# One array layout (64 rows by 32 columns, two lanes) for the matmuls of an attention-plus-MLP kernel

## The chip, the cores and the metric

The kernel runs on one core of a Trainium2 chip. The metric is device time in microseconds of one execution; the number shown is the median of three runs. One further execution was recorded by the hardware profiler, and all views of the profile come from it. The engines are TensorE (PE in the profile; its weight loads are listed as PEld), ScalarE (ACT), VectorE (DVE), GpSimd (POOL) and SyncE (SP, which here only issues DMAs).

## The reference

The input `x` has 2048 tokens of 640 features. It is layer-normed, and the result `xn` feeds two branches whose outputs are added to `x`:

```python
xn = layernorm(x)                              # 2048 x 640
# A: 32 query heads of 20 features, one shared key head and one shared value head
scores = (xn @ wq per head) @ (xn @ wk).T * 20 ** -0.5
o = softmax(scores) @ (xn @ wv);   a = concat(o) @ wo
# B
b = silu(xn @ w1) @ w2                         # 640 -> 1728 -> 640
out = x + a + b
```

The scores are 32 heads x 2048 queries x 2048 keys, some 134 million exponentials; they are never stored, only their product with the values is.

## The kernel before

**Tiling of attention.** The queries are cut into 4 chunks of 512 (`QW`), the heads into 8 groups of 4 (`HG`). That gives 32 groups `g`, and each meets 16 key tiles `kt` of 128 keys. One unit of work is one head of one (g, kt): a score matmul with K = 20 features padded to 32, giving 128 keys x 512 queries in one PSUM bank (`s_mm`, line 1002; the matmul has the line L1003 in the profile). There are 32 x 16 x 4 = 2048 such units. The exponential of a unit goes one of two ways:

- on ScalarE, two or three units in one instruction over neighbouring banks (`make_s_act`, line 1057; the exponential is L1094). One matmul pass with the values then follows per (g, kt) (`make_pv_act`).
- on VectorE, always the four heads of a (g, kt), called a *batch* (`dve_items`, `dve_job`, `dve_advance`). The exponential is built by integer arithmetic on the bf16 bit pattern: four instructions that move a bank to SBUF (L1285, named p1), one shifted copy on VectorE (L1326), one on GpSimd (L1321). The three variants are added up by three value passes in place of one.

A value pass (`pv_mms`, L1129) is four matmuls, one for each head, side by side in the columns of the array; all accumulate in PSUM bank 7 (`UB`) until the group is complete, then VectorE copies the sum out (L1177).

**Dense work.** The q projections (`q_job`), the first MLP layer (`h_job`, `h_pair`; tanh on ScalarE, L709, product on VectorE, L712), and the second layer together with the output projection (`out_job`, `y_job`, and `fin_job` at the end) use `col_mm` (L395): four matmuls of 32 output columns each, side by side, repeated over chunks of the contracted dimension into one bank.

**Layouts of the array.** A matmul names its place in the 128 x 128 array. Three layouts occur, called modes in the code:

- "s": 32 rows x 128 columns, for the scores. Up to four heads run at once.
- "p": 128 rows x 32 columns, for values and dense work. The four side-by-side matmuls run at once.
- "f": the whole array, for transposes, k, v and the first q, mostly in the first 50 us.

**The order.** The program is not written out by hand. A planner (`Sched`, `step_pe`, `pe_candidates`, `plan`) steps through a modelled time and always commits the next instruction of the engine that is furthest behind. The matmul engine has a list of candidates: scores for ScalarE ("s"), scores for VectorE ("d"), values ("p", and "pd" for batches), dense jobs ("m", "l"). The planner holds costs (`t_mc`, `t_act`, `t_dve`) and `SWITCH`, the price of a change of layout; a table of rules chosen by a letter for each 10 us (`RULES`, `PLAN`) alters its thresholds. The finished order is fixed at build time; `emit` adds semaphore waits, one semaphore for each engine, and none from TensorE to itself. Work is shared between ScalarE and VectorE by the planner too: a batch is claimed (`claim`) when VectorE can be given one. PSUM has 8 banks, one for the values and seven for scores and dense jobs; exponentials wait in `Ebuf` (`NSLOT` = 20 slots of 512 columns).

**The start and the end.** The first scores need kT, which is written by one copy per job (`kT_job`, L566 and L568) into `kT_rep`: the same keys four times, once for each head's 32 rows. After the last exponential come the last value passes, the normalization of the last group through two small matmul stages (L924 and L942), the `fin_job` passes (L395) and the last additions (L891).

Of the kernel before, what the change touches and what calls it, by code (L numbers as in the profile page):

```python
# [8 lines left out]
BF16 = mybir.dt.bfloat16  # L9
# [5 lines left out]
P = 128  # L15
# [4 lines left out]
SLOT = 32  # L20
HG = 4
NG = H // HG
# [17 lines left out]
NSLOT = 20  # L40
# [4 lines left out]
NQS = 3  # L45
# [4 lines left out]
WAITS = 0.0  # L50
BUSY = 0.5
STRETCH = 2400.0
FILLGAP2 = 120.0
FILL = 0.7
WARM = 2400.0
# [14 lines left out]
SWITCH = 105.0  # L70
# [7 lines left out]
FIN_ACT = ()  # L78
# [10 lines left out]
BASE = dict(lagmax=6, lagp=0, lagj=6, openlag=3, late=-0.02, lead=0.01, leadmax=0.02, need=500.0, hold=300.0, dwant=600.0, slack=700.0, dnow=400.0, hungry=0.0, patience=0.0, keep=460.0, open=2, zcap=9, stay=0.0, homes=1, last=6, twin=2, spare=300.0, want=1, claim=6)  # L89
RULES = dict(a={}, b=dict(keep=0.0), c=dict(lagp=3), d=dict(lagp=5), e=dict(lagp=0), f=dict(patience=200.0), g=dict(dwant=0.0),  # L90
             h=dict(zcap=4), i=dict(zcap=3), j=dict(homes=0), k=dict(leadmax=-1.0, lead=-1.0), l=dict(lead=0.08, leadmax=0.1),
             m=dict(need=560.0), n=dict(hold=0.0), o=dict(stay=460.0), p=dict(open=1), q=dict(slack=400.0), r=dict(hungry=1000.0), s=dict(claim=9), t=dict(open=3), u=dict(claim=4), v=dict(want=2), w=dict(twin=0), x=dict(need=440.0), y=dict(last=9), z=dict(last=6, hungry=1000.0))
PLAN = "bcbngdnvnroonapqndntaiaoinqqahppinxaaopfcfahhprpppopddmimdqahjqooafogaa"


def rule(n):
    return PLAN[n] if n < len(PLAN) else "a"
# [13 lines left out]
class Op:  # L111
    __slots__ = ("eng", "fn", "occ", "lat", "pre", "reads", "writes", "prio", "mode", "slots",
                 "start", "fin", "done", "deps", "inc", "job", "first", "last", "gate", "on_commit", "seq", "name",
                 "dma_sem", "dma_val", "port", "run")

    def __init__(self, eng, fn, occ, lat=0.0, pre=(), reads=(), writes=(), prio=5.0, mode=None, slots=None,
# [10 lines left out]
        self.slots = slots  # L127
# [12 lines left out]
        self.run = None  # L140
# [10 lines left out]
def t_mc(n):  # L151
    return n / 2.4 + (9.0 if n >= 512 else 4.0)
# [6 lines left out]
class Job:  # L159


    def __init__(self, name, cost):
        self.name = name
        self.cost = cost
        self.bank = None
        self.mms = deque()
        self.consumers = []
        self.ready = None
        self.fixed = None
        self.head = None  # L170
        self.batch = None


class Piece:


    def __init__(self, job, mms=None):
        self.job = job
        self.mms = deque(job.mms if mms is None else mms)
        self.gate = job.gate  # L180
        self.kind = None


class Sched:
    ENG = ("pe", "act", "dve", "pool", "sp")

    def __init__(self):
# [4 lines left out]
        self.pe_set = None  # L192
# [22 lines left out]
    def est(self, op):  # L215
# [6 lines left out]
        if op.slots is not None and self.joined(op) is not None:  # L222
            t = self.pe_set[0] + 4.0 * len(self.pe_set[1])
# [10 lines left out]
    def joined(self, op):  # L234

        if op.slots is None or self.pe_set is None or op.slots & self.pe_set[1] or self.t["pe"] > self.pe_set[2] + 1.0:
            return None
        return self.pe_set[0]

    def commit(self, op, start):  # L240
        e = op.eng
        op.deps = self.hazards(op)
        op.start = start
        if e == "pe":
            if op.mode != self.pe_mode:
                start += SWITCH + (10.0 if op.mode == "p" and self.pe_mode != "s" else -3.0 if op.mode == "p" else 0.0)
                self.pe_mode = op.mode
            s0 = self.joined(op)
            if s0 is not None:
                end = max(start + op.occ, self.pe_set[2])  # L250
                self.pe_set = (s0, self.pe_set[1] | op.slots, end)
                op.fin = start + op.occ + (142.0 if op.run else 170.0)
                op.occ = end - self.t[e]
                self.t[e] = end
            else:
                op.fin = start + op.occ + (142.0 if op.run else 170.0)
                self.t[e] = start + op.occ
                self.pe_set = (start, op.slots, start + op.occ) if op.slots else None
# [21 lines left out]
def build(nc, A_x, A_wq, A_wk, A_wv, A_wo, B_x, B_w1, B_w2, out, stack):  # L280
# [33 lines left out]
    kT_rep = sb([P, S], BF16)  # L314
# [76 lines left out]
    def col_mm(pe, b, n, w, x, start, stop, off=0):  # L391

        ins = None
        for j in range(w.shape[-1] // SLOT):
            ins = pe.matmul(ps[j * SLOT:(j + 1) * SLOT, b * BANK + off:b * BANK + off + n], w[:, j * SLOT:(j + 1) * SLOT], x,  # L395
                            start=start, stop=stop, tile_position=(0, j * SLOT))
        return ins

    def pe_job(name, mms, cost, gate=None):

        job = Job(name, cost)
        for k, (fn, occ, mode, pre, reads) in enumerate(mms):
            op = Op("pe", fn, occ, pre=pre, reads=reads, mode=mode, job=job, name=name)
            op.first = k == 0
            op.last = k == len(mms) - 1
            job.mms.append(op)
        job.ops = list(job.mms)
        job.ready = job.ops[-1]
# [21 lines left out]
    pool(lambda g: g.memset(mhalf[:, :], -0.5), 120, writes=[res("mh")], prio=0.03)  # L430
    idb = pool(lambda g: g.tensor_copy(ident_b[:, :], ident_f[:, :]), 290, reads=[res("idf")], writes=[res("idb")],
# [1523 lines left out]
```

## Time and profile before

| what | value |
|---|---|
| median of three runs | 706.66 us (706.38 to 706.92) |
| span of the profiled execution | 704.7 us |
| PE busy | 688.3 us, 98% |
| ACT busy | 683.8 us, 97% |
| DVE busy | 618.6 us, 88% |
| POOL busy | 363.6 us, 52% |
| matmuls / weight loads | 9915 / 9915 |
| exponentials on ScalarE | 665 instructions (583 of two units, 82 of three) |
| batches on VectorE | 159 |

The span of the profiled execution is 2.0 us under the median of the runs. How to read the views: a group row gives line, engine, operation, shapes and count, then the busy time and the mean duration of one, then the idle time just before them and what ended it. Instructions of an engine overlap at their ends, so that the mean duration is more than the step from one start to the next. For a matmul the shape "32*128" is rows times columns of the array that it uses. A timeline row gives start and length in us; neighbouring instructions of one group are merged, with their count behind the x.

### The profile page before, as it was taken

Reading aid. Unit: us, or ns where it says so; the run is one execution under the profiler, and the core shown is the slowest. Engines: PE = TensorE matmul, PEld = TensorE weight load, DVE = VectorE, ACT = ScalarE, POOL = GpSimd, SP = SyncE. Lnnn points to the kernel's source line nnn. Section 1 sums busy time; section 2 is a strip of 40 time slices with the busy share of each in tenths; the row PEclk is TensorE's granted clock in tenths of the full one; section 3 lists DMA queues with packets and bytes.
Section 4 is the critical chain, followed back from the end, with each engine's and each line's share of the span. In section 5 each row is a group of like instructions: output and inputs, shape, how many; then the busy total and the mean of one; then the engine's idle time right before and its main releaser. Section 6 shows DMA issues by size and latency. Waiting matters only on the chain.

```text
span 704.7 us, 22677 instructions
## 1 busy us (share of the span) xinstructions
PE 688.3 (98%) x9915; PEld 231.3 (33%) x9915; DVE 618.6 (88%) x1067; ACT 683.8 (97%) x737; POOL 363.6 (52%) x235
## 2 busy tenths in 40 slices
PE   7999999999999999999999999999999999999998
PEld 5432323222223333322222333332222333333345
DVE  7789999999998998889988899898999898889893
ACT  6999999999999999999999999999999999999993
POOL 6625544565565555445545446565554555455551
PEclk9999999999999999999999999999999999999999
DMA  8643220322221122323112222033222112232201
GB/s 222 196 145 40 21 19 19 31 29 26 21 24 16 29 40 30 65 28 33 17 19 29 28 31 30 19 62 43 30 20 20 18 21 33 28 68 24 21 8 39
DMA packets 34241, 28.97 MB, mean 41 GB/s; under 512 B 15486, under 2 KB 29662, under 8 KB 34142
## 3 DMA queue, kind: packets, MB, share of 16 engines
q1 hardware_dynamic: 33854, 27.20, 25.2%
q8 instruction: 77, 1.26, 0.8%
q10 hardware_dynamic: 288, 0.33, 0.1%
q14 instruction: 22, 0.18, 0.1%
HBM read 11.09 MB, written 2.62 MB: 19 GB/s over the span
## 4 chain that ended last, share of the span: by engine, by line
ACT 65%; PE 31%; DVE 2%; DMA 1%; POOL 0%; issue 0%; SPq 0%; POOLq 0%
ACT sbt L1094 63%; PE psall L1003 10%; PE psall L1129 10%; PE psall L395 9%; ACT sbt L709 3%; DMA sbt<-in_A_wq_dram 1%; PE psall L558 0%; PE psall L1608 0%; PE psall L924 0%; PE psall L942 0%; DVE sbt L500 0%; PE psall L670 0%; DVE sbt L1285 0%; DVE sbt L891 0%; PE psall L532 0%
## 5 line engine op out<-in xcount | busy, mean ns | idle before, releaser
L1094 ACT ACTIVATE sbt<-psall 128x1024 bf16<-128x1024 f32 (+1 forms) x665 | 661.2, 1223 | 3.4 <-PE psall L1003 2.9
L1285 DVE TENSOR_SCALAR sbt<-psall 128x512 int16<-128x512 f32 x636 | 417.2, 683 | 57.3 <-PE psall L1003 54.0
L1321 POOL TENSOR_SCALAR sbt<-sbt 128x2048 int16<-128x2048 int16 x159 | 302.0, 1899 | 300.0 <-DVE sbt L1326 116.2
L1003 PE MATMUL psall<-sbt 32*128 32x512 bf16 x2048 | 269.0, 384 | 7.6 <-ACT sbt L1094 3.8
L1129 PE MATMUL psall<-sbt 128*32 128x512 bf16 x3320 | 263.2, 384 | 1.6 <-DVE sbt L1177 1.1
L395 PE MATMUL psall<-sbt 128*32 128x320 bf16 (+3 forms) x3904 | 232.0, 331 | 0.3 <-DVE sbt L712 0.3
L1003 PEld LDWEIGHTS psall<-sbt 32*128 32x128 bf16 x2048 | 70.9, 91 | 254.0 <-ACT sbt L1094 189.5
L1326 DVE TENSOR_SCALAR sbt<-sbt 128x2048 int16<-128x2048 int16 x159 | 110.2, 704 | 1.8
L395 PEld LDWEIGHTS psall<-sbt 128*32 128x32 bf16 (+1 forms) x3904 | 83.9, 95 | 83.7 <-issue 51.6
L1129 PEld LDWEIGHTS psall<-sbt 128*32 128x32 bf16 x3320 | 66.1, 94 | 113.7 <-issue 79.8
L789 POOL TENSOR_TENSOR sbt<-sbt 128x512 bf16<-128x512 f32 x30 | 38.3, 1276 | 11.9 <-DVE sbt L1326 8.5
L712 DVE SCALAR_TENSOR_TENSOR sbt<-sbt,psall 128x512 bf16<-128x512 bf16 x52 | 35.5, 682 | 3.0 <-ACT sbt L709 2.6
L709 ACT ACTIVATE sbt<-psall 128x512 bf16<-128x512 f32 x52 | 37.8, 727 | 0.0
L1177 DVE COPY sbt<-psall 128x512 f32<-128x512 f32 x31 | 21.1, 680 | 0.1
L1608 PE MATMUL psall<-sbt 128*32 128x256 bf16 (+1 forms) x308 | 19.1, 338 | 1.2 <-DVE sbt L424 1.2
L630 DVE TENSOR_SCALAR sbt<-psall 128x512 bf16<-128x512 f32 x20 | 13.7, 685 | 1.2 <-PE psall L395 0.7
L831 DVE SCALAR_TENSOR_TENSOR sbt<-psall,sbt 128x320 bf16<-128x320 f32 x24 | 11.6, 482 | 0.5 <-PE psall L395 0.4
L522 POOL TENSOR_SCALAR sbt<-sbt 128x640 bf16<-128x640 bf16 x12 | 10.4, 879 | 2.5 <-DVE sbt L514 2.4
L1608 PEld LDWEIGHTS psall<-sbt 128*32 128x32 bf16 x308 | 8.2, 105 | 6.0 <-issue 2.5
L846 DVE SCALAR_TENSOR_TENSOR sbt<-psall,sbt 128x320 f32<-128x320 f32 x8 | 3.9, 485 | 6.4 <-PE psall L395 6.3
L532 PE MATMUL psall<-sbt 128*128 128x128 bf16 x80 | 7.1, 221 | 1.6 <-DVE sbt L525 1.1
L509 POOL TENSOR_TENSOR sbt<-sbt 128x2 f32<-128x2 f32 x8 | 5.6, 694 | 5.8 <-DVE sbt L507 5.7
(61 smaller groups left out, 98.9 us busy)
## 6 DMA issues: line engine op xcount, KB each, us to landing
sbt<-sbt SPq DMA_DIRECT2D x120, 64.0 KB, 3.9
sbt<-in_A_x_dram SPq DMA_DIRECT2D x28, 160.0 KB, 4.1
sbt<-sbt SPq DMA_DIRECT2D x213, 20.0 KB
out_dram<-sbt SPq DMA_DIRECT2D x14, 160.0 KB, 2.0
sbt<-in_B_w_dram SPq DMA_DIRECT2D x1, 2160.0 KB, 10.4
sbt<-in_B_w_dram SPq DMA_DIRECT2D x1, 2080.0 KB, 8.1
sbt<-sbt SPq DMA_DIRECT2D x75, 8.0 KB
sbt<-in_A_wq_dram SPq DMA_DIRECT2D x1, 800.0 KB, 6.7
```

What stands on the lines that cost most here:

```text
L395: ins = pe.matmul(ps[j * SLOT:(j + 1) * SLOT, b * BANK + off:b * BANK + off + n], w[:, j * SLOT:(j + 1) * SLOT], x, start=start, stop=stop ...
L709: t = Op("act", lambda a: a.activation(t_buf[0:rows, ts, :], bk(job.bank, 0, QW, rows=rows), AF.Tanh, scale=0.5), t_act(512), 215, pre=[jo ...
L712: u = Op("dve", lambda v: v.scalar_tensor_tensor(out=hT[par][0:rows, fk, :], in0=t_buf[0:rows, ts, :], scalar=1.0, in1=bk(job.bank, 0, QW, ...
L789: nm = pool(lambda e: e.tensor_tensor(oU[:, us, :], U_sb[:, us, :], Rrep, ALU.mult), 1350.0 + MARGIN, pre=[uc] + lc + pack_op.get(divmod(g ...
L1003: return pe.matmul(bk(b), kT_rep[i * SLOT:(i + 1) * SLOT, kt * P:(kt + 1) * P], qT[i * SLOT:(i + 1) * SLOT, g % NQ, :], start=True, stop=T ...
L1094: return a.activation(Ebuf[:, es * QW:es * QW + w], ps[:, buf[0] * BANK:buf[0] * BANK + w], AF.Exp, scale=ESCALE)
L1129: ins = pe.matmul(ps[i * SLOT:(i + 1) * SLOT, UB * BANK:UB * BANK + QW], lhsT, rhs, start=(first and k < HG), stop=(last and k >= len(lst) ...
L1177: uc = Op("dve", lambda v: v.tensor_copy(U_sb[:, us, :], bk(UB)), t_dve(512), 140, pre=[pv] + up, reads=[sc.banks[UB]], writes=[res("U", u ...
L1285: p1 = Op("dve", lambda v: v.tensor_scalar(z16[:, i * QW:(i + 1) * QW], bk(job.bank), ZBIAS, 0.0, ALU.add, ALU.max), t_dve(QW), 140, pre=[ ...
L1321: op = pool(lambda v, t=t, j=j, zin=zin: v.tensor_scalar(t.bitcast(I16), zin, float(SHIFT[j]), 1.0, ALU.add, ALU.mult), POOL_SHIFT, prio=0 ...
L1326: op = dve(lambda v, t=t, j=j, zin=zin: v.tensor_scalar_add(t.bitcast(I16), zin, float(SHIFT[j])), t_dve(N, 4), prio=SPRIO - 0.01 * j, **args)
L1608: ins = pe.matmul(ps[i * SLOT:(i + 1) * SLOT, UB * BANK:UB * BANK + n], zero_t[:, 0:SLOT], zero_t[:, 0:n], start=fresh, stop=fresh, tile_p ...
```

## The change

All score, value and dense matmuls use one layout: 64 rows x 32 columns. The array then has two *lanes* (the upper and the lower 64 rows, `rg` 0 and 1) of four column places each.

- **Scores.** A unit becomes four matmuls of 32 keys each, in the lane that holds its head (heads 0 and 1 in lane 0, heads 2 and 3 in lane 1). As a lane holds two heads' rows, kT is kept twice (`kT_ab`): one copy has zeros in the rows of the odd heads, the other in those of the even ones. A mask multiplies the copies in; the second copy waits for the first, as both read one bank.
- **Values and dense work.** Each pass of four matmuls becomes two half passes, over the upper and the lower 64 rows of the contracted dimension, in lanes 0 and 1.
- **Two lanes and one bank.** Both lanes add into the same bank for a value group or a dense job. Where the lane changes, the planner puts a wait of TensorE on its own earlier matmul (`blocked`, `selfwait`); TensorE has two semaphores for that, one for each lane.
- **The planner.** `rgfree` holds when each lane is free. Values stay in one lane until it is `runmax` half passes ahead. ScalarE is given two units at a time (`tri=0`); at most two banks wait for VectorE (`dmax=2`). `RULES`, `PLAN`, the twin sets and the fillers between scores are gone. `fin_job` passes are pieces of two half passes each.
- **Memory.** `NSLOT` 20 to 18, `NQS` 3 to 2.
- **Small work.** The zeroing of the ragged rows of `hT` on GpSimd goes; the last MLP chunk uses only the lane that holds data; VectorE zeroes a strip of `oT` and writes the mask.

```diff
-NSLOT = 20
+NSLOT = 18
-NQS = 3
+NQS = 2
-SWITCH = 105.0
+SWITCH = 100.0
+BASE = dict(lagmax=6, lead=0.01, leadmax=0.02, open=2, zcap=9, last=6, claim=6, dmax=2, runmax=4, linger=240.0, tri=0, need=700.0)
...
 def t_mc(n):
-    return n / 2.4 + (9.0 if n >= 512 else 4.0)
+    return n / 2.4 + 3.0
...
+    def blocked(self, op, bank):
+        w = self.acc.get(bank)
+        return w if w is not None and w.rg != op.rg else None
...
-    def col_mm(pe, b, n, w, x, start, stop, off=0):
+    def col_mm(pe, b, n, h, w, x, start, stop, off=0):
         ins = None
+        lo, hi = h * HROW, (h + 1) * HROW
         for j in range(w.shape[-1] // SLOT):
-            ins = pe.matmul(ps[j * SLOT:(j + 1) * SLOT, ...], w[:, j * SLOT:(j + 1) * SLOT], x,
-                            start=start, stop=stop, tile_position=(0, j * SLOT))
+            ins = pe.matmul(ps[j * SLOT:(j + 1) * SLOT, ...], w[lo:hi, j * SLOT:(j + 1) * SLOT], x[lo:hi],
+                            start=start, stop=stop, tile_position=(lo, j * SLOT))
...
+        for k in range(2):
+            args = dict(pre=[*job.ready, *mask_ops] + ops, writes=[res("kT", i, k) for i in range(t0, t1)], job=job)
+            if t0 == 1 or k == 1:
+                op = Op("dve", lambda v, k=k: v.tensor_scalar_mul(dst[:, k, :], bk(job.bank, 0, n), mask[:, k:k + 1]), ...)
+            else:
+                op = Op("act", lambda a, k=k: a.activation(dst[:, k, :], bk(job.bank, 0, n), AF.Copy, scale=mask[:, k:k + 1]), ...)
+            ops.append(op)
...
     def s_mm(pe, b, g, kt, i):
-        return pe.matmul(bk(b), kT_rep[i * SLOT:(i + 1) * SLOT, kt * P:(kt + 1) * P],
-                         qT[i * SLOT:(i + 1) * SLOT, g % NQ, :], start=True, stop=True, tile_position=(i * SLOT, 0))
+        r = slice(i // 2 * HROW, (i // 2 + 1) * HROW)
+        for c in range(P // SLOT):
+            k = kt * P + c * SLOT
+            ins = pe.matmul(bk(b)[c * SLOT:(c + 1) * SLOT], kT_ab[r, i % 2, k:k + SLOT], qT[r, g % NQ, :], start=True, stop=True,
+                            tile_position=(i // 2 * HROW, c * SLOT))
+        return ins
...
+        u = u_lane[0]
+        near = [min((e for _, e in x.values()), default=1e12) for x in pv]
+        if (near[u] > t + ru.linger or (pv_ahead[0] if u else -pv_ahead[0]) >= ru.runmax) and near[1 - u] <= t + ru.linger:
+            u = u_lane[0] = 1 - u
...
+        if not pro and xbanks() and dve_held(t) < ru.dmax:
+            for r in range(2):
+                dj = dve_items(r)
...
+            w = sc.blocked(op, bank) if bank is not None else None
+            if w is not None:
+                e = max(e, w.fin + LAT)
...
+        order = ["s", "m0", "d"] + (["p", "pd", "m", "l"] if lag_now() >= ru.lagmax else ["m", "p", "pd", "l"])
+        best = min(rd, key=lambda x: (order.index(x[0]), x[2])) if rd else None
```

More of the change, by code (lines that the diff above doesn't have):

```diff
@@ L242, in commit @@
         op.deps = self.hazards(op)
+        if op.selfwait is not None:
+            op.deps.add(op.selfwait)
         op.start = start
@@ L550, in build, with kT_res @@
     kT_op = {}
+    def kT_res(kt):
+        return [res("kT", kt, k) for k in range(2)]
     def kT_job(t0, t1):
@@ L1214, in z_idle @@
         b = z_last[k]
-        return b is None or b["pv"] is not None and all(o.done for o in b["pv"])
+        return b is None or b["pv"] is not None and all(o.done for x in b["pv"] for o in x)
     def z_slot():
@@ L1255, in dve_items @@
                 open_b.append(st)
-                pick = next(((st, j) for j in st["left"] if j not in busy), None)
-        if pick is None and open_b:
-            pick = open_b[0], open_b[0]["left"][0]
+                pick = next(((st, j) for j in st["left"] if j // 2 == r), None)
         if pick is None:
@@ L1811, in emit @@
                     continue
-                if d.eng == e and e == "pe":
+                if d.eng == e and e == "pe" and d is not op.selfwait:
                     continue
```

747 lines of the change are left out of this document (336 added, 411 removed).

## The prediction

> **What bounds the kernel now.** I read the page's busy shares first, then the groups with shapes kept apart, the stages, the waits, and last the timeline of single stretches.
>
> ```profile
> PE 688.3 (98%) x9915; PEld 231.3 (33%) x9915; DVE 618.6 (88%) x1067; ACT 683.8 (97%) x737; POOL 363.6 (52%) x235
> ```
>
> ```profile
> L1094 ACT ACTIVATE sbt<-psall 128x1024 bf16<-128x1024 f32 x583 | 565.8, 1174 | 0.7 <-PE psall L1003 0.5
> L1285 DVE TENSOR_SCALAR sbt<-psall 128x512 int16<-128x512 f32 x636 | 417.2, 683 | 57.3 <-PE psall L1003 54.0
> ...
> L1003 PE MATMUL psall<-sbt 32*128 32x512 bf16 x2048 | 269.0, 384 | 7.6 <-ACT sbt L1094 3.8 <-DVE sbt L1285 0.7 <-ACT sbt L568 0.3
> L1129 PE MATMUL psall<-sbt 128*32 128x512 bf16 x3320 | 263.2, 384 | 1.6 <-DVE sbt L1177 1.1 <-DVE sbt L1326 0.2 <-ACT sbt L1094 0.2
> L1094 ACT ACTIVATE sbt<-psall 128x1536 bf16<-128x1536 f32 x82 | 127.5, 1573 | 2.7 <-PE psall L1003 2.4
> L395 PE MATMUL psall<-sbt 128*32 128x512 bf16 x1468 | 114.5, 383 | 0.3 <-DVE sbt L712 0.3
> L395 PE MATMUL psall<-sbt 128*32 128x320 bf16 x2320 | 114.5, 301 | 0.0
> ```
>
> ```profile
> 50.00:200.00 150.00, 147.89 (x1918) 44.58 (x1910) 141.97 (x235) 149.08 (x172) 79.15 (x44) 1.00 0.23 25
> 200.00:350.00 150.00, 146.84 (x2114) 46.39 (x2111) 134.16 (x221) 149.93 (x159) 79.27 (x45) 1.00 0.25 32
> 350.00:500.00 150.00, 148.95 (x2118) 46.49 (x2118) 132.60 (x220) 150.00 (x162) 79.11 (x44) 1.00 0.25 32
> 500.00:650.00 150.00, 147.45 (x2214) 49.02 (x2206) 132.53 (x218) 149.97 (x160) 78.36 (x47) 1.00 0.24 29
> ```
>
> The columns of the stages are length, PE, PEld, DVE, ACT, POOL, clock and DMA. ScalarE never rests from 200 to 650 us, so the time falls only if it gets fewer exponentials, that is, if VectorE takes more batches. VectorE has room: 399.3 of 450 us there. The groups say why it rests: 54.0 of the 57.3 us before p1 (L1285) go to scores that TensorE has not delivered.
>
> And TensorE has no time to deliver them:
>
> ```profile
> 300.15 0.39 PE L1003 MATMUL psall<-sbt 32*128 32x512 bf16 x2
> 300.47 0.40 PE L1129 MATMUL psall<-sbt 128*32 128x512 bf16 x4
> 300.70 0.39 PE L395 MATMUL psall<-sbt 128*32 128x512 bf16 x4
> 301.02 0.39 PE L1003 MATMUL psall<-sbt 32*128 32x512 bf16 x3
> ```
>
> ```profile
> 160.13 1.26 PE L1129 MATMUL psall<-sbt 128*32 128x512 bf16 x20
> ```
>
> ```profile
> PEld psall L1003 <- ACT sbt L1094: 189.5, 496, 1.2
> ...
> PEld psall L1129 <- issue: 79.8, 352, 0.2
> PEld psall L395 <- issue: 51.6, 227, 0.4
> PEld psall L1003 <- issue: 31.0, 93, 0.5
> ```
>
> Five value passes of four matmuls take 1.26 us, the last 0.38 of it being one matmul's length: a step of 0.22 per pass. But from the scores at 300.15 to the next layout it is 0.32, and from the pass at 300.70 back to scores 0.32 again: 0.10 more each time. The waits count the changes: 496 + 93 = 589 entries into the score layout and 352 + 227 = 579 out of it, 1168 x 0.10 = 117 us. With scores (some 600 sets x 0.22 = 132), values (830 passes x 0.22 = 183), dense (367 x 0.22 + 580 x 0.14 = 162) and the whole-array work that is 610 us, and the smaller rows of waits hold more changes. TensorE, ScalarE and the order are all at their limit at once.
>
> **The change, part by part.** Durations are of the profiled execution (704.7 us); the median of the runs is 2.0 us above it, and I add that at the end.
>
> ```profile
> L532 PE MATMUL psall<-sbt 128*128 128x128 bf16 x80 | 7.1, 221 | 1.6 <-DVE sbt L525 1.1 <-DVE sbt L630 0.5
> L558 PE MATMUL psall<-sbt 128*128 128x512 bf16 x15 | 3.9, 382 | 0.0
> L582 PE MATMUL psall<-sbt 128*128 128x32 bf16 x80 | 2.6, 176 | 0.0
> L605 PE MATMUL psall<-sbt 128*128 128x128 bf16 x20 | 1.8, 220 | 0.7 <-DVE sbt L544 0.6
> ```
>
> ```profile
> 13.12 0.39 PE L1003 MATMUL psall<-sbt 32*128 32x512 bf16 x3
> 13.45 0.66 PE L582 MATMUL psall<-sbt 128*128 128x32 bf16 x20
> 13.56 1.45 ACT L1094 ACTIVATE sbt<-psall 128x1536 bf16<-128x1536 f32 x1 [0.63 <-PE psall L1003]
> ```
>
> ```profile
> 689.56 0.39 PE L1003 MATMUL psall<-sbt 32*128 32x512 bf16 x3
> ...
> 694.50 1.95 PE L942 MATMUL psall<-sbt 128*32 128x128 f32 x64
> 696.27 5.10 PE L395 MATMUL psall<-sbt 128*32 128x128 bf16 x144
> ```
>
> *TensorE's sum.* The changes of layout go, save those of the first 50 us. A unit of scores now fills a lane of its own for one pass, so 2048 units need 2048 / 2 x 0.22 = 225 us, where sets of three or four heads needed 132. Values and dense work stay at 183 and 162: twice the half passes, two at a time. With some 15 us of whole-array work (the first four rows) the sum is 585 us. Scores run from 13.1 to 689.6 us, 676 us. TensorE would be busy 87% of that. So about 13% comes free, provided that both lanes can be kept at work; the first rival is that they can't.
>
> ```profile
> 50.52 0.46 PE L1003 MATMUL psall<-sbt 32*128 32x512 bf16 x4
> ```
>
> That two sets in different rows may start at different times, which the lanes need, is seen here, too: four score matmuls in 0.46 us, where one takes 0.39, so the later ones started some 0.07 late into a running array.
>
> ```profile
> 88.99 3.84 ACT L1094 ACTIVATE sbt<-psall 128x1024 bf16<-128x1024 f32 x4
> 92.71 0.62 ACT L709 ACTIVATE sbt<-psall 128x512 bf16<-128x512 f32 x1
> 93.19 3.81 ACT L1094 ACTIVATE sbt<-psall 128x1024 bf16<-128x1024 f32 x4
> ```
>
> ```profile
> 299.74 1.29 DVE L1285 TENSOR_SCALAR sbt<-psall 128x512 int16<-128x512 f32 x2 [0.59 <-PE psall L1003]
> ```
>
> *More batches (the gain).* On ScalarE four exponentials of two units step from 88.99 to 92.71, 0.93 each, so four heads cost 1.86 us. On VectorE two p1 take 1.29, one 0.68: a step of 0.61, and a batch of four p1 and a shift 5 x 0.61 = 3.05. A batch that moves shortens the span by 1.86 and fills 3.05 of VectorE, so r us of recovered idle time move r / 4.91 batches. At most r = 54 (11 batches, 20.5 us). Nearest below: the stage from 50 to 200 us, where VectorE is at 94.6%; bringing the 450 us after it from 88.7% to that gives r = 27 (5.4 batches, 10.1 us). I take the middle, r = 40: 8.1 batches, 15.2 us off. No gain at all is rival three.
>
> *Pairs only.* 82 exponentials of three units become 123 of two: 41 more instructions. By mean durations (1174 and 1573) the third unit costs 0.40, the fixed part is 0.38, and 41 of it 15 us; but by busy time a unit costs 565.8 / 1166 = 0.485 in pairs and 127.5 / 246 = 0.518 in threes, a gain. The steps decide: one unit (92.71 to 93.19) takes 0.48, two 0.93, so the fixed part is 0.03: 1.2 us.
>
> *kT twice.* The first scores wait for a second copy on VectorE: between 0 (hidden) and 0.7 us (one p1 of the same width, 0.68), I take 0.5. The four later ones, 0.68 each, sit on VectorE while scores are short: 2.7 us there are worth 2.7 / 4.91 x 1.86 = 1.0. Together 1.5.
>
> *The end.* All 36 `fin_job` passes stand in the tail, 5.10 us. Each becomes two half passes that must not overlap, with a lane change between. Its price: scores at 13.12 of 0.39 length release the exponential at 13.56, and of the 0.44 us 0.22 is the pass: a change costs 0.22. If all 36 stay in the tail it is 36 x 0.22 plus their streaming once more (4.8): 12.7 us. If the freed TensorE does the 20 that need no last group sooner, 2.8 are saved. I take only the last pass of each of the five banks, 5 x (0.22 + 0.21) = 2.1.
>
> *At nothing:* the mask and the strip of zeros on VectorE (six small writes; uncovered under 1 us), GpSimd's zeroing (GpSimd is half idle), fewer `Ebuf` and q slots (if the values lag by nine pairs, ScalarE stops; part of rival one), and the loss of `PLAN`, of which no row shows the worth: the range carries it.
>
> *Sum:* 704.7 - 15.2 + 1.2 + 1.5 + 2.1 = 694.3, and 2.0 to the median: **696 us**.
>
> **Rivals.**
>
> *One, slower: the lanes lock each other out.* Values need 2 x 183 us of lane time and, with 1660 half passes in runs of eight, 208 lane changes of 0.22, 46 us; dense work 2 x 162, and 106 jobs with a change each, 23 us. Each of the two can be in one lane only at any time, as it adds into one bank. Scores take a third of each lane, so the two need (412 + 347) / 0.67 = 1133 us inside a window of 676 at par: they must be in opposite lanes 68% of the time. A dense job starts in the lane that is free and ends in the other, where the values are if they have not moved: apart between half and three quarters of the time. At 68% the time is as before, with the small costs; at 60% the window is 1133 / 1.6 = 708, 32 more: 739 us. For it: the narrow margin, and work queued behind each wait of TensorE on itself, on an engine that issues in order. Against it: scores for VectorE may go to whichever lane is idle. The Trainium skill, "TensorEngine Tiling (Array Packing)", section "Gotcha 1: PSUM Pressure", says that different row tiles cannot use one bank at the same time and that software must see to it. No run here shows it: each score matmul writes a bank of its own.
>
> ```profile
> 696.27 0.41 PE L395 MATMUL psall<-sbt 128*32 128x128 bf16 x16
> ```
>
> *Two, slower: issue.* Matmuls become 8192 + 6640 + some 7700, with a load each: 45,000 instructions, 14.6 ns for each in 660 us. The tail shows 64 matmuls with 64 loads in 1.95 us, at most 15.2 ns each, and for a short while 16 matmuls in 0.41 - 0.22, 6 ns an instruction. The trace shows no slower limit, but no long stretch at this rate either, and the queue may have been full before. At 16 ns: 720, 28.7 at both ends and 2.0: 751 us.
>
> The v matmuls start 25 ns apart ((0.66 - 0.18) / 19). The skill's "TensorE: Matmul & The Clock Gate", section "Wait — 56ns, not 53.3ns?", makes 25 ns the floor from start to start of any matmul. By it eight passes of 320 columns' width would need 0.20 in place of 0.14 and dense work 35 us more, 620 us of TensorE in all; the steps of (0.41 - 0.22) / 15, 13 ns, in the row above speak against that where matmuls lie side by side.
>
> *Three, about the same: VectorE isn't fed better.* Two banks may wait for it, and a bank's round is 0.22 of scores, 0.22 of release, 0.68 of p1 and a release back of some 0.2: 1.32, so 0.66 for each p1 against a step of 0.61. With a quarter of the idle time recovered (13 us, 5 off) and the same costs: 706 us.
>
> **How the numbers follow.** Forecast 0.45 (its own range 684 to 703), rival one 0.35, rival three 0.12, rival two 0.08. Rival three spreads over 702 to 711. A change under 0.2% can't be told from none here (the runs lie within 0.54 us). Faster: 0.45 + 0.02 = 0.47; within 0.2%: 0.06 of rival three and 0.01 of the others, 0.07; slower: 0.46. The range 681 to 750 leaves out the far ends of rivals one and two and a little below.
>
> **What would show it.** No changes of layout between 50 and 690 us; scores steps of 0.22 with eight matmuls; 163 to 170 batches (L1285 over 650 instructions); idle time before p1 under 30 us; ScalarE still above 97%. Rival one: ScalarE idle before exponentials and TensorE's waits put down to TensorE itself or long idle lanes. Rival two: matmul starts evenly spaced, with "issue" as the releaser. Rival three: the batch count at 159 to 162 with TensorE idle. The forecast is wrong above all if both lanes together stay under 85% in use.

## The result: slower by 13.5%

The changed kernel takes 804.15 us (median of four runs, 800.22 to 813.39) against 706.79 us for the kernel before on the same chip: a ratio of 1.1353, 95% interval 1.1313 to 1.1393. All ratios here leave out an execution that is over 1.5% above the fastest of its kernel (here the one of 813.39 us), so that 1.1353 is a little below 804.15 / 706.79. The prediction said 696 us and a range of 681 to 750. The profiled execution has a span of 798.3 us, 93.6 more than before.

The page and the groups with shapes apart, of the kernel after:

```profile
PE 757.1 (95%) x23083; PEld 404.8 (51%) x23083; DVE 630.2 (79%) x1098; ACT 688.9 (86%) x765; POOL 369.8 (46%) x235
...
q8 instruction: 180, 2.95, 1.6%
```

```profile
L1126 ACT ACTIVATE sbt<-psall 128x1024 bf16<-128x1024 f32 x683 | 650.5, 1081 | 55.9 <-PE psall L1035 53.3 <-PE psall L1158 1.0
L1158 PE MATMUL psall<-sbt 64*32 64x512 bf16 x6704 | 511.9, 378 | 8.7 <-issue 6.1 <-DVE sbt L1206 0.5 <-DVE sbt L1347 0.2
L1035 PE MATMUL psall<-sbt 64*32 64x512 bf16 x8192 | 507.3, 381 | 16.6 <-issue 10.4 <-DVE sbt L601 3.0 <-ACT sbt L1126 1.2
L1306 DVE TENSOR_SCALAR sbt<-psall 128x512 int16<-128x512 f32 x652 | 423.3, 684 | 69.8 <-PE psall L1035 63.5 <-PE psall L410 1.9
...
L410 PE MATMUL psall<-sbt 64*32 64x512 bf16 x2952 | 227.8, 383 | 1.0
L410 PE MATMUL psall<-sbt 64*32 64x320 bf16 x4512 | 224.3, 299 | 6.2 <-issue 5.5
```

L1126 is the exponential (L1094 before), L1306 p1 (L1285), L1035 the scores, L1158 the values, L410 dense work. No other layout is left in the rows of scores, values and dense work, and each matmul lasts as long as before (378 to 383 ns for 512 columns, 299 for 320). So the array did what it was asked to. But ScalarE, which almost never rested, now stands idle 55.9 us before exponentials of two units, 53.3 of it for scores, where it was 0.7, and VectorE's idle time before p1, which was to fall below 30 us, rose from 57.3 to 69.8. Batches rose by four only (652 / 4 = 163).

The stages, in the columns of those shown before:

```profile
50.00:200.00 150.00, 148.49 (x4255) 68.53 (x4247) 136.49 (x225) 144.65 (x166) 73.41 (x42) 1.00 0.22 26
200.00:350.00 150.00, 141.89 (x4656) 80.24 (x4636) 119.13 (x197) 135.41 (x149) 72.44 (x41) 0.99 0.23 30
350.00:500.00 150.00, 143.82 (x4639) 78.20 (x4631) 127.29 (x212) 139.09 (x156) 74.27 (x42) 1.00 0.23 28
500.00:650.00 150.00, 144.58 (x4579) 76.39 (x4559) 128.94 (x216) 139.06 (x156) 79.54 (x47) 1.00 0.22 30
650.00:770.00 120.00, 112.44 (x3924) 74.65 (x3917) 79.96 (x136) 95.68 (x103) 47.99 (x27) 1.00 0.19 26
770.00:798.00 28.00, 22.93 (x268) 4.47 (x260) 3.46 (x5) 0.00 (x0) 0.00 (x0) 0.50 0.07 25
```

Two things stand out. From 200 us on even TensorE has idle time (8.1 us of 150 in the worst stage; 1 to 3 before), though it is what all others wait for. And there is a stage of 28 us at the end without any exponential, at a granted clock of 0.50. The last exponential ends at 757.7 us (692.1 before), so that 65.6 us were lost in the main part and 28.0 after it (40.6 from there to the end of the span, 12.6 before).

The list of waits:

```profile
ACT sbt L1126 <- PE psall L1035: 56.9, 81, 2.2
...
PEld psall L410 <- PE psall L410: 32.0, 72, 1.0
...
PEld psall L1158 <- PE psall L1158: 28.5, 81, 0.6
...
PEld psall L1035 <- issue: 21.2, 29, 2.3
...
PEld psall L410 <- issue: 13.4, 25, 2.3
PEld psall L1158 <- issue: 12.6, 16, 2.2
```

TensorE waits for itself: dense work for dense work, values for values. These are lane changes within one bank, rival one. And it waits for nothing the profile shows ("issue"), in few but long pieces of up to 2.3 us. The timeline of one of them:

```profile
295.63 0.38 PE L1158 MATMUL psall<-sbt 64*32 64x512 bf16 x3
297.76 0.09 PEld L1158 LDWEIGHTS psall<-sbt 64*32 64x32 bf16 x1 [2.25 <-issue]
297.76 0.39 PE L1158 MATMUL psall<-sbt 64*32 64x512 bf16 x1 [1.75 <-issue]
```

A value half pass is four matmuls without a wait between them. Here three run, and the fourth and its load come 2.1 us later. No semaphore can cut a pass in two at that place. The transfers of instructions can: the page counts 180 packets on q8 (77 before), and TensorE issues 2 x 23,083 = 46,166 loads and matmuls, 256 for each packet. The trace has a packet that starts at 289.73 us, the next only at 295.36, and work goes on at 297.76, 2.4 us after that start. Between 40 and 757 us there are 62 gaps in TensorE's starts of over 0.3 us that end on an instruction without a wait; beyond a pass of 0.22 they hold 31.4 us, 28.5 of it from 240 to 340, 440 to 510 and 610 to 757 us, where the 320-column passes run. Before, packets came 9.15 us apart on average, and no gap without a wait was longer than 0.5 us.

So three theories went into the experiments. **L**, the lanes lock each other out. **F**, TensorE's instructions aren't delivered fast enough. **T**, the end is a chain of half passes that can't overlap. A rival, **R**, is that two lanes at once are slower in the array itself.

### The profile page after: what moved, and what is told of

Its sections match the earlier page's. It is cut to its first block, busy times and chain, and to the rows that moved or that the text cites. A ratio compares the mean times of both kernels' runs of the same rounds, so it can differ in the third digit from the quotient of the medians.

```text
span 798.3 us, 49725 instructions
## 1 busy us (share of the span) xinstructions
PE 757.1 (95%) x23083; PEld 404.8 (51%) x23083; DVE 630.2 (79%) x1098; ACT 688.9 (86%) x765; POOL 369.8 (46%) x235
## 4 chain that ended last, share of the span: by engine, by line
PE 89%; DVE 4%; issue 4%; ACT 2%; DMA 1%; POOL 0%; SPq 0%; POOLq 0%
PE psall L1035 32%; PE psall L1158 30%; PE psall L410 24%; ACT sbt L1126 2%; DVE sbt L1306 1%; DMA sbt<-in_A_x_dram 1%; PE psall L561 0%; PE psall L591 0%; DVE sbt L1347 0%; DVE sbt L601 0%; DVE sbt L573 0%; DVE sbt L1206 0%; PE psall L972 0%; ACT sbt L745 0%; PE psall L707 0%
## 5 line engine op out<-in xcount | busy, mean ns | idle before, releaser
L1126 ACT ACTIVATE sbt<-psall 128x1024 bf16<-128x1024 f32 (+1 forms) x693 | 663.5, 1086 | 59.5 <-PE psall L1035 56.9
L1035 PE MATMUL psall<-sbt 64*32 64x512 bf16 x8192 | 507.3, 381 | 16.6 <-issue 10.4
L1158 PE MATMUL psall<-sbt 64*32 64x512 bf16 x6704 | 511.9, 378 | 8.7 <-issue 6.1
L1306 DVE TENSOR_SCALAR sbt<-psall 128x512 int16<-128x512 f32 x652 | 423.3, 684 | 69.8 <-PE psall L1035 63.5
L1342 POOL TENSOR_SCALAR sbt<-sbt 128x2048 int16<-128x2048 int16 x163 | 309.2, 1897 | 358.8 <-PE psall L1158 202.9
L410 PE MATMUL psall<-sbt 64*32 64x320 bf16 (+3 forms) x7680 | 465.9, 334 | 9.0 <-issue 5.5
L1035 PEld LDWEIGHTS psall<-sbt 64*32 64x32 bf16 x8192 | 158.1, 90 | 170.6 <-ACT sbt L1126 71.5
L410 PEld LDWEIGHTS psall<-sbt 64*32 64x32 bf16 x7680 | 187.7, 92 | 102.0 <-PE psall L410 32.0
L1158 PEld LDWEIGHTS psall<-sbt 64*32 64x32 bf16 x6704 | 172.5, 91 | 98.5 <-PE psall L1158 28.5
L1347 DVE TENSOR_SCALAR sbt<-sbt 128x2048 int16<-128x2048 int16 x163 | 112.2, 697 | 33.0 <-PE psall L1158 32.5
L745 ACT ACTIVATE sbt<-psall 128x512 bf16<-128x512 f32 x52 | 36.0, 691 | 0.0
L920 DVE SCALAR_TENSOR_TENSOR sbt<-psall,sbt 128x512 bf16<-128x512 f32 x5 | 3.5, 691 | 22.9 <-PE psall L410 22.9
L666 DVE TENSOR_SCALAR sbt<-psall 128x512 bf16<-128x512 f32 x20 | 13.6, 682 | 4.2 <-PE psall L410 4.2
L573 DVE COPY sbt<-psall 128x640 bf16<-128x640 bf16 x14 | 6.6, 485 | 4.3 <-PE psall L561 4.3
```

The lines of the kernel that those rows point to most:

```text
L666: op = Op("dve", lambda v: v.tensor_scalar_mul(q_st[:, st, :], bk(job.bank), QSCALE), t_dve(512), 140, pre=[*job.ready], writes=[res("qst" ...
L745: t = Op("act", lambda a: a.activation(t_buf[0:rows, ts, :], bk(job.bank, 0, QW, rows=rows), AF.Tanh, scale=0.5), t_act(512), 215, pre=[*j ...
L1035: ins = pe.matmul(bk(b)[c * SLOT:(c + 1) * SLOT], kT_ab[r, i % 2, k:k + SLOT], qT[r, g % NQ, :], start=True, stop=True, tile_position=(i / ...
L1126: return a.activation(Ebuf[:, es * QW:es * QW + w], ps[:, buf[0] * BANK:buf[0] * BANK + w], AF.Exp, scale=ESCALE)
L1158: ins = pe.matmul(ps[i * SLOT:(i + 1) * SLOT, UB * BANK:UB * BANK + QW], lhsT[r], rhs[r], start=first, stop=last, tile_position=(h * HROW, ...
L1306: p1 = Op("dve", lambda v: v.tensor_scalar(z16[:, i * QW:(i + 1) * QW], bk(job.bank), ZBIAS, 0.0, ALU.add, ALU.max), t_dve(QW), 140, pre=[ ...
```

## The experiments

A ratio is to the kernel before on the same chip. "Main" is where the last exponential ends in the profiled execution, "end" what the span has after it; for the kernel without locks the profiled execution is that of 786.17 us. Where two runs lie too far apart, no interval is given.

| kernel | time | ratio, 95% interval | main | end |
|---|---|---|---|---|
| before | 706.79 | 1 | 692.1 | 12.6 |
| after | 804.15 | 1.1353 (1.1313 to 1.1393) | 757.7 | 40.6 |
| half the tiles in out and y jobs | 765.56 | 1.0817 (1.0759 to 1.0876) | 724.7 | 37.5 |
| no locks | 777.65 (769.13, 786.17) | none given | 754.6 | 29.6 |
| no locks, half the tiles | 719.65 | 1.0169 (1.0131 to 1.0207) | 697.7 | 19.5 |
| full-height end | 782.29 | 1.1054 (1.0907 to 1.1201) | 765.7 | 18.9 |
| grouped end | 794.35 | 1.1223 (1.1158 to 1.1287) | 758.0 | 36.1 |
| wide dense tiles | 1567.75 (1499.51, 1635.99) | none given | | |
| before, untuned | 717.05 | 1.0144 (1.0124 to 1.0163) | 700.8 | 14.4 |
| before, cut in 2 | 711.07 | 1.0052 (1.0040 to 1.0064) | 694.2 | 14.7 |
| before, cut in 3 | 794.27 | 1.1221 (1.1132 to 1.1311) | 770.0 | 19.9 |
| before, cut in 4 | 994.71 | 1.4053 (1.3944 to 1.4162) | 968.1 | 27.8 |

### Fewer instructions, the same passes

```diff
-  return col_mm(..., h, hT[par][:, fk, i * P:(i + 1) * P], w2_sb[...], ...)
+  return col_mm(..., h, hT[par][:, fk, i * P:i * P + P // 2], w2_sb[...], ...)
...   (the same for oT in o_mms; the fin jobs keep all four)
```

> Theory F (TensorE's instructions are not delivered fast enough where passes are 320 columns wide) against theory L (the lanes lock each other out) and R (two lanes at once are slower in the array). This kernel leaves out two of the four column tiles in every half pass of the out and y jobs: half of the second product and of the output projection is not computed. Passes, lanes, banks, waits and the order stay; 2,256 matmuls and as many loads go, all from the phases with 320 columns. F: the gaps without any wait that I find in the trace after (62 over 0.3 us between 40 and 757 us, 31.4 us beyond a pass's length) go, the last exponential comes 30 to 36 us sooner, 768 to 774 us. L and R: 800 to 806 us, since a half pass lasts as long with two tiles as with four.

Measured: 765.56 us. The last exponential comes 33.0 us sooner (757.7 to 724.7), and of the gaps without a wait 4.7 us are left before it. ScalarE's wait has halved:

```profile
L1126 ACT ACTIVATE sbt<-psall 128x1024 bf16<-128x1024 f32 x683 | 644.7, 1092 | 28.1 <-PE psall L1035 25.1 <-PE psall L410 2.4
```

The exponentials, batches and waits on itself are the same in number or nearly so (27.8 and 27.0 us); only 4,512 of 46,166 loads and matmuls are gone. That is F, and it is worth 1.1353 - 1.0817 = 0.054, 38 us. A small part of it may be the granted clock, on average 0.98 in the kernel after and 0.985 here. R alone would have left the time where it was.

### No locks, and both together

```diff
-  job.passes.append([half_mm(job, fn, h, occ, pre, reads) for h in range(2)])
+  job.passes.append([half_mm(job, fn, 1, occ, pre, reads) for h in range(2)])
...
-            op.rg = h
+            op.rg = 0            # values (pv_ops_of)
```

> This kernel puts both half passes of the values in lane 0 (rows 0 to 63 twice, rows 64 to 127 left out) and both of all dense work in lane 1 (rows 64 to 127 twice), so that no bank is ever added to from both lanes. Count and length of all matmuls stay. L: ScalarE's idle time before exponentials falls from 59.5 us to under 15, TensorE's waits on itself (28.5 and 32.0 us) go, some 45 us off the main part, and the lane changes of the end go too (70 half passes at 0.37 us become some 0.2): 804 - 45 - 12 = 747 us, between 735 and 760. F adds that the same instructions are then wanted in less time, so its stalls stay at 30 us or grow. R, or an array too busy in itself: still over 790 us.

> Both edits together. L and F as separate causes that add: 747 less 30 to 36, 711 to 717 us, near the kernel before. F alone: as with half tiles, 768 to 774. L alone: as without locks, about 747. If the stalls only filled time that the locks left idle, the two together give less than the sum of both.

Measured: 777.65 us without locks and 719.65 with both edits. The two executions of the first missed its 747 by 22 and 39 us; their mean granted clocks are 0.997 and 0.983. Its waits on itself are gone, but "issue" has taken their place:

```profile
ACT sbt L1126 <- PE psall L1035: 68.2, 96, 2.3
...
PEld psall L410 <- issue: 42.3, 81, 2.3
...
PEld psall L1035 <- issue: 25.5, 27, 2.6
PEld psall L1158 <- issue: 20.3, 23, 2.4
```

Its gaps without a wait hold 57.3 us (in the execution of 786.17 us), where the kernel after had 31.4. The expectation let F stay at 30 "or grow" and put no number on the growth; that was the mistake. With half the tiles on top, the gaps are down to 6.7 us and the time is near that of the kernel before. Groups of that last kernel:

```profile
L1126 ACT ACTIVATE sbt<-psall 128x1024 bf16<-128x1024 f32 x666 | 627.9, 1113 | 20.6 <-PE psall L1035 19.6 <-PE psall L410 0.5
...
L1306 DVE TENSOR_SCALAR sbt<-psall 128x512 int16<-128x512 f32 x688 | 447.1, 684 | 28.5 <-PE psall L1035 21.2 <-PE psall L410 2.4 <-PE psall L1158 0.2
```

So both causes are real, and they hide one another. With F out of the way, L costs 1.0817 - 1.0169 = 0.065, 46 us: 27.0 of it in the main part (724.7 to 697.7) and 18.0 in the end (37.5 to 19.5). Up to 9 of those 18 are the granted clock and not the locks, as the section on the end shows, and without locks the planner also found another order, with nine batches more; so L is 37 to 46 us. With L in the way F costs 38 us. Without it, it costs 49 (769.13 to 719.65, the two executions whose clocks are alike, 0.997 and 1.000). Lanes that wait less want their instructions faster. For R at most the last 12 us are left (0.0169).

### The positive control: more instructions in the kernel before

```diff
+CUT = 2                # 3, 4
...
-        for j in range(w.shape[-1] // SLOT):
+        for lo, hi, j in ((q * n // CUT, (q + 1) * n // CUT, j) for q in range(CUT) for j in range(w.shape[-1] // SLOT)):
...    (the matmul takes columns lo to hi; the same in pv_mms)
```

> The kernel before, with each matmul of the values and of the dense jobs cut in two halves of its columns (256 or 160 wide), each with its load; array work, order, banks and waits are the same. Matmuls 9,915 to 17,139; by the matmuls of the trace before, 42 to 62 instructions per us in every stretch of 50 us. F: the trace after shows blocks of 256 instructions fetched no closer than 3.3 to 3.45 us, 74 to 78 per us; 62 stays below, so 707 to 712 us. A price on each matmul (rival two of the prediction) would show here: at 1.4 ns more for each of 14,400 new instructions, 20 us. R (the array slower with lanes) says 707.

> The same in three parts (170 or 106 wide): 24,363 matmuls, 48,700 instructions, about as many as the kernel after has. By stretches of 50 us 59 to 90 per us; five of them lie above 76. F: what lies above costs some 21 us if nothing else comes late, and blocks that are asked for late add to it: 725 to 755 us, with gaps of 1.5 to 2.5 us without a wait as in the trace after. The spacing of starts alone (13 ns between neighbours, four tiles of 106 columns want 11): 13 us, 720. No limit: 708.

> The same in four parts (128 or 80 wide): 31,587 matmuls, 63,174 instructions, 76 to 117 per us. F: the delivery sets the time, 63,174 x 3.4 / 256 = 839 us, 830 to 880 us, with the fetches evenly spaced at 3.3 to 3.5 us. If only the spacing of starts counts (13 ns against 8 where 80 columns are cut four ways): 580 passes x 16 x 13 ns less 133 ns each, 43 us more, 750 us. With no limit at all 708.

Measured: 711.07, 794.27 and 994.71 us. With twice the instructions, up to 60 per us in the densest 50 us of its trace, the kernel before is 0.5% slower, so there is hardly a price on each matmul. Cut in three, the kernel before has about as many instructions as the kernel after, no lanes at all, and takes nearly as long. That is 39 us above the upper end of what F was expected to give, and cut in four it is 115 above. Gaps of over 0.5 us in TensorE's starts that end on an instruction without a wait (between 40 us and the end of the main part, or 955 us in the last) show the cause: none in the kernel before, 2 cut in two, 62 cut in three, 209 cut in four, with 52 and 195 us beyond a pass in the last two. The groups and the waits of the kernel cut in four show the same picture, made large:

```profile
L1095 ACT ACTIVATE sbt<-psall 128x1024 bf16<-128x1024 f32 x583 | 572.8, 1032 | 204.3 <-PE psall L1004 202.3
```

```profile
PEld psall L396 <- issue: 191.0, 328, 3.0
PEld psall L1131 <- issue: 172.6, 431, 2.8
...
PE psall L396 <- issue: 118.9, 94, 2.9
...
PE psall L1131 <- issue: 66.0, 70, 2.6
```

Why the expectation was too low is seen in the distances between the instruction packets on q8 (50 us after the start to 40 us before the end):

```
                      packets   5% under   mean   closest ten in a row, mean
before                     77    6.60 us   9.15   7.95
before, cut in 2          134    3.51      5.23   4.43
before, cut in 3          190    3.37      4.07   3.77
before, cut in 4          247    3.38      3.95   3.75
after                     180    3.39      4.19   3.72
after, no locks           181    3.39      4.15   3.65
after, half the tiles     163    3.46      4.43   4.20
```

A single packet can follow after 3.4 us, but now and then one comes a further 1 to 2.5 us late (after: 5.71 us behind the one at 627.39, 4.46 at 654.98, 5.58 at 681.02, 3.4 to 3.8 between most others; cut in four, 37 of 229 come after more than 4.4). Ten in a row never took less than 3.65 us each: 70 instructions per us, 14.3 ns each, and over the kernel cut in four 15.4 ns (3.95 us / 256). I had put in 3.4. The granted clock averaged 0.92 in that run, but it is not what limits it: 1639 matmuls came between 200 and 250 us at 1.00, 1575 between 850 and 900 at 0.80. In part the late ones fall where data is moved: of the 56 packets in whose first 3.4 us the other queues kept more than two DMA engines busy, 25 were followed late, of the other 173 only 12. That the transfers hold them up is not shown. The Trainium skill, "Runtime: NRT & Kernel Launch", section "Instruction fetch mechanics", says that instructions come in blocks of 256 through a DMA queue of the sequencer's own, the next while the current one is executed, and that crossing a block is mostly hidden. The trace agrees on the 256. At 28 instructions per us it agrees on the rest too; near 70 it doesn't.

### The end

```diff
-            mms += o_mms(qc, i, d0, d1, range(YC[i], DC - 1), off)
+            mms += [(f, occ, "p", pre, rd) for f, occ, _, pre, rd in o_mms(qc, i, d0, d1, range(YC[i], DC - 1), off)]
...    (in col_mm, rows 0 to 127 for these; the same for the passes of fin_step)
```

> The last passes (fin jobs: all three kinds) go back to 128 rows by 32 columns, one pass where there were two half passes; nothing else changes. Theory T (the end is a chain of lane changes): TensorE's work after 769 us, 280 matmuls in 26.2 us, becomes 140 in 36 passes of at most 0.22, 8 us, and the layout changes add one or two: 16 to 19 us off, 785 to 788 us. If the end is slow only because the clock is granted at 0.50 there: at most 26.2 / 2 = 13 off if the clock comes back, and nearly nothing if it does not, 791 to 804.

```diff
-        for k in range(len(job.passes) - 1, 0, -1):
-            misc_front.insert(at + 1, Piece(job, job.passes[k:k + 1]))
-        return Piece(job, job.passes[:1])
+        return Piece(job)
...    (the same in fin_c)
```

> The kernel after, with the last passes of a bank handed to the order in two pieces instead of one by one, so that all passes of one lane come before those of the other: 64-row tiles stay, but lane changes in the end fall from one per pass to some three per bank, 70 to about 20. If the end is bound by lane changes and these cost the same as before: 50 fewer at 0.22 less the 0.1 of streaming that they hide, 8 to 11 us off the 26.2. If it is bound by the clock of 0.50 that is granted there: the passes themselves (70 of at most 0.43 at half the clock) stay, and less than 6 us come off. The main part is untouched but its stalls fall differently, 5 us either way.

Measured: 782.29 us with full height, 794.35 grouped. In the profiled executions the end falls from 40.6 us to 18.9 and 36.1; with full height the main part is 8.0 us longer, which the edit doesn't explain. The last TensorE rows of five timelines, the kernel after, full height, grouped, no locks, no locks with half the tiles:

```profile
767.57 0.55 PE L410 MATMUL psall<-sbt 64*32 64x128 bf16 x8
...
769.05 26.19 PE L410 MATMUL psall<-sbt 64*32 64x128 bf16 x280
```

```profile
776.27 5.01 PE L410 MATMUL psall<-sbt 128*32 128x128 bf16 x140
```

```profile
768.10 3.02 PE L410 MATMUL psall<-sbt 64*32 64x128 bf16 x64
771.06 1.94 PE L972 MATMUL psall<-sbt 128*32 128x128 f32 x32
772.92 18.11 PE L410 MATMUL psall<-sbt 64*32 64x128 bf16 x224
```

```profile
761.98 19.17 PE L410 MATMUL psall<-sbt 64*32 64x128 bf16 x280
```

```profile
704.26 9.85 PE L410 MATMUL psall<-sbt 64*32 64x128 bf16 x280
```

35 full passes take 0.143 us each at a clock of 1.00. The 70 half passes take 0.374 each, nearly all at 0.50. The two kernels without locks stream the same 70 half passes in one lane, without a lane change (the fin jobs keep all four tiles there): 19.17 us at 0.50 (from 761.5 us on) and 9.85 us at 1.00. So the way from 26.19 us to 5.01 divides into 7.0 for lane changes, 9.3 for the clock alone and 4.8 for twice as many passes. Grouping removes most lane changes, and by the rows (0.55 + 26.19 against 3.02 + 18.11) brings 5.6 us; the clock stays at 0.50. It was under 6 that I had written down for the clock as the cause: it is the largest of the three parts, and T is right for the other two. Another 5.7 us are lost ahead of these passes: the first starts 9.9 us after the last exponential, 4.2 before.

The grant falls to 0.50 at 769.5 us in the kernel after and at 769.1 in the grouped one; with full height it stays at 1.00. One lane at work is not the reason by itself, as the last row is one lane alone at 1.00 (until 716.8 us). It also differs between executions of one kernel: without locks the mean clock is 0.983 in the profiled one and 0.997 in the other, which leaves the other some 5 us at 0.50 (an estimate: 0.003 x 767 / 0.5). Why the clock falls stays open.

### A wider tile, and the side parts

```diff
-        for j in range(w.shape[-1] // SLOT):
-            ins = pe.matmul(ps[j * SLOT:..., ...], w[lo:hi, j * SLOT:(j + 1) * SLOT], x[lo:hi], ..., tile_position=(lo, j * SLOT))
+        return pe.matmul(ps[:, ...], w[lo:hi, :], x[lo:hi], start=start, stop=stop, tile_position=(lo, 0))
```

> The kernel after, with each half pass of dense work as one matmul of 64 rows by 128 columns where there were four of 64 by 32: the same rows, lanes, banks, waits and result; some 5,700 matmuls and as many loads fewer. F: like the half tiles, and nothing is left out: 760 to 772 us. If a tile of another width beside 32-wide tiles costs a change of layout (0.10 us each before), every one of some 1,900 half passes may pay it, and the time goes over 850 us.

Measured: 1499.51 and 1635.99 us, though a quarter of the instructions are gone. The timeline:

```profile
301.64 0.39 PE L1155 MATMUL psall<-sbt 64*32 64x512 bf16 x4
301.96 0.39 PE L409 MATMUL psall<-sbt 64*128 64x512 bf16 x1
302.27 0.40 PE L1032 MATMUL psall<-sbt 64*32 64x512 bf16 x4
```

Each dense half pass starts 0.32 after the work in front of it and 0.31 ahead of the next, with nothing running in the other lane: a change of layout by the step that the trace before showed (0.32 in place of 0.22), now twice for each half pass, and the two lanes one after the other. But that is not the whole loss. Two of its stages:

```profile
300.00:350.00 50.00, 49.28 (x742) 15.57 (x744) 29.48 (x48) 36.08 (x40) 13.25 (x8) 1.00 0.09 10
450.00:500.00 50.00, 50.00 (x383) 10.91 (x379) 13.21 (x22) 14.34 (x14) 6.97 (x4) 0.50 0.09 10
```

The granted clock is 0.50 from 375 to 1266 us (mean 0.70, and 0.78 in the other execution). Between 50 and 350 us, at 1.00, 579 units had their exponential, or its first step on VectorE, and 848 in the kernel after: at that pace the main part would take 1.46 times as long, some 1110 us (an estimate from these counts). The rest is the clock, and what lowered it is not shown. So the remedy for F, fewer and wider matmuls, is not to be had beside 32-column tiles, at full clock either.

```diff
-NSLOT = 20          -NQS = 3          -PLAN = "bcbngdnvnroo..."
+NSLOT = 18          +NQS = 2          +PLAN = ""
```

> The kernel before with three side parts of the change and not the layout: the written-out string of rules (PLAN) emptied, Ebuf at 18 slots, two q staging slots. My prediction put these at nothing within its range. If they are nothing: 704 to 709 us. If the string of rules carries part of the loss: 712 to 725 us; the lanes and the supply then explain that much less.

Measured: 717.05 us, ratio 1.0144: 10 us. The side parts are not nothing. It is close to the 0.0169 (12 us) by which the kernel without locks and with half the tiles still stands above the kernel before; that the two are the same loss was not tried.

**The sum.** 38 us for delivery, 46 for locks (18 of them in the end, up to 9 of these the clock) and 12 for the rest make 96, which is 0.1353 of 706.8; that it comes out is no check, as each is the difference of two neighbours in one row of kernels. The full-height end brings 21 back (1.1353 to 1.1054, with an interval of 0.015 either way). No version here beats the kernel before: even where locks and late instructions are taken away by leaving work out, it is 1.7% slower.

## Why the prediction was wrong

**The step that failed first is *TensorE's sum*, in its proviso**: "about 13% comes free, provided that both lanes can be kept at work". The array time was right: by the same step of 0.22 for eight matmuls, scores are 225 us, values 6704 / 8 x 0.22 = 184, dense work 2952 / 8 x 0.22 + 4512 / 8 x 0.14 = 160, and each matmul kept its length. But these 569 us stand in a main part of 757.7 - 12.6 = 745 from the first scores on: 76% in use, not 87%. What stands in the way is shown above: TensorE waits where a lane changes within one bank, and it waits for instructions. The prediction's own mark for being wrong was 85%. The kernel without locks and late instructions reaches (225 + 188 + 160) / (697.7 - 12.0) = 84%.

**Rival one** (0.35) had the mechanism: the waits of TensorE on itself, and 27 us in the main part where it priced 32 at 60%; that the two are close is luck, as 60% was only a case. It was too low, because it counted nothing for the end and nothing for instructions.

**Rival two** (0.08) was dismissed, and that was the worst call. Its 16 ns for an instruction is what the long run gives (15.4 cut in four; 14.3 at best), against a need of 14.6. The page of before even lists instruction packets, 77 on q8. The evidence I set against it, 64 matmuls in 1.95 us and 16 in 0.19, were bursts of 128 and 32 instructions, less than one packet of 256, which can run from what has been fetched before. "The queue may have been full before" stood in the text and is the likely answer. Nor did I ask what the mean hides: stretches of 10 us without 320-column passes start 50 to 65 instructions per us, those with them up to 76, and nearly all of the time is lost there (28.5 of 31.4 us). Even the sum itself asked for too much: sixteen instructions in each 0.22 us are 73 per us while both lanes are full. What it was to show, evenly spaced starts, was wrong too: the loss comes in gaps of 2 us.

***The end*** was put at 2.1 us, with 12.7 as the upper bound; it was 28.0. The bound had the second streaming (4.8, measured 4.8) and the lane changes (7.9, measured 7.0) right. It took the passes at full clock, which is 9.3 us, and had nothing for the 5.7 us ahead of them; and TensorE did none of the passes sooner.

***At nothing* for the loss of `PLAN`**, with fewer slots, was 10 us in the kernel before.

***More batches***: the forecast was 8.1 more, there were 4 (163), and 13 (688 / 4 = 172) once locks and late instructions were gone. The trade was nearly right: ScalarE's busy time fell to 665.9 us there, 17.9 less than before, where 13 x 1.86 is 24. It brought nothing, since ScalarE was no longer what the time hung on (the chain that ended last is 84% TensorE there and 4% ScalarE). *kT twice* cost nothing to see: the first exponential starts at 13.23 us, 13.56 before. *Pairs only* was not measured by itself.

**Rival three** would have had TensorE idle with few batches; the batches stayed few, but because scores came late.

The 25 ns from start to start that the Trainium skill states ("TensorE: Matmul & The Clock Gate", section "Wait — 56ns, not 53.3ns?"), weighed against the trace in rival two, don't hold between tiles side by side: a row of eight score matmuls in both lanes takes 0.41 us where one lasts 0.38, so all eight start within 0.03.

```profile
754.36 0.41 PE L1035 MATMUL psall<-sbt 64*32 64x512 bf16 x8
```

## What to carry to other kernels

A free share of an engine is only worth something if the work that is to fill it can be there: two lanes that add into one bank are one lane for that work, and a sum of array time doesn't see it. Whoever cuts matmuls into smaller tiles should divide the instructions of TensorE by the time of each phase, not of the kernel; here about 70 per us was all that a stretch of 2,560 could get, and 60 was still all but free. A price that is taken from a burst says nothing of a rate that must be held.

## What the hardware showed that I had not expected

- TensorE stands still for up to 2.3 us, in the middle of a pass and without any wait, when its next 256 instructions come late (3.0 in the kernel cut in four). Work goes on some 2.2 to 2.5 us after the packet starts, and packets start no closer than 3.2 us, ten in a row no closer than 3.65 us each. Why some come later than the others was not found.
- A row of 64-row, 32-column tiles runs in both lanes at full speed (0.41 us for eight matmuls), but one 64 x 128 matmul among them stops both lanes: 0.32 us from start to start.
- The granted clock fell to 0.50 with TensorE listed as busy 13.6 of 15 us (770 to 785 us, the kernel after), and with wide tiles it stood there for 890 us with TensorE busy all the time (50.00 of 50 us). The same 280 matmuls took 19.17 us at 0.50 and 9.85 at 1.00. Which of the two an execution gets was not found.
